# Unit scales on ACT, another order of the first readers, a two-column maximum, and a reordered opening in a conv, GELU and rational MLP kernel

## The chip, the cores and the metric

One core of one Trainium2 chip runs the whole program. The metric is the device time of one execution in microseconds, as the median of several runs; lower is better. The engines are PE (TensorE, with its weight loads PEld), DVE (VectorE), ACT (ScalarE), POOL (GpSimd) and SP (SyncE).

## The reference

```python
# 1. causal 7-tap convolution over the sequence, taps = softmax(weight), one set of taps per head
x_pad = np.concatenate([np.zeros((B, 6, 192)), x], axis=1)
out = np.einsum('hk,bskhg->bshg', w, x_unf)        # x: (2, 4096, 192) -> 8192 tokens x 192
# 2. first MLP: sigmoid-GELU
h = x @ w_in;  g = h * (1 / (1 + np.exp(-1.702 * h)));  x = g @ w_out        # d_ff = 2048
# 3. second MLP: a rational function of h
h = x @ w_in2
P = a[0] + a[1]*h + a[2]*h**2 + a[3]*h**3
Q = 1 + abs(b[0])*abs(h) + abs(b[1])*h**2
out = (P / (Q + 1e-06)) @ w_out2
```

## The kernel before

The 8192 tokens are cut into 16 blocks of 512. The hidden width 2048 is 16 chunks of 128, worked on in eight pairs (index i), one pair to a PSUM tile of 128 x 1024. For precision most products are made from fp16 parts: a tensor is scaled by a power of two, ACT writes its high half (`high_part`, `g1_high`, `split`), DVE writes the rest (`low_part`, `g1_low`), and PE multiplies high and low parts in three terms (`h_main`, `h_side`, `o1_product`). The scale of a tensor comes from its maximum: DVE reduces each partition (`x2_red_part`, in two parts, and L554 joins them), PE turns that column into a row on every partition (`all_max`, L85), DVE takes the maximum of the row (L89) and makes the scale (`scales`).

The main loop goes over j, the block whose second MLP runs, and n1 = j + 1, the block whose first MLP runs.

- **The front part** (`front_groups`, or `front_phase` for j = 0) makes the eight hidden pairs of both MLPs. For the first MLP ACT does the GELU (L524) and the high half (L534), DVE the low half (L538). For the second, `unit` has ACT write |h| (L585) and a linear term (L586), DVE two steps of the polynomial (L587, L588), then `denominator` (L593). The h products lie in a ring of three PSUM tiles (`ps_h`); a tile comes free when its last reader has ended. `front_groups` takes the products in groups of three. The first group was multiplied ahead, at the end of the iteration before: two first-MLP products (`early`, called e0 and e1 here) and one second-MLP product (`second`, called s0). Its readers come in the order e0, s0, e1.
- **The back part** (`back_phase`) multiplies out the first MLP (L496, L506), while POOL makes the convolution of block j + 3 from seven taps (L328, L332; only for j up to 12, since there are 16 blocks). Behind it come x2's maximum and scale, x2's two halves (L345, L348), the group e0, e1, s0 ahead for the next iteration, and part of the second MLP's output products (L485, two passes of fp32). `x2_scales` (L573) makes four small columns, each from the one before it, that `unit` needs as scales of the next block; they are POOL instructions and stand in POOL's queue behind the convolution.
- **The opening** (`prologue`) splits the weights, and runs the first MLP of block 0 with unsplit weights (`o1_whole`: L496 and L506 in turn for each chunk), after which x2 of block 0 is made in the same way. Four `w_out1_split` make the fp16 parts of w_out1; DVE has a step in each (L213), ACT another (L212).
- **The ending** (`ending`) has the last block alone.

The order of each engine's instructions is mostly the order of the text (`manual_schedule`); waits and PSUM slots are placed by the framework.

Of the kernel before, what the change touches and what calls it, by code (L numbers as in the profile page):

```python
# [20 lines left out]
def kernel(  # L21
# [52 lines left out]
    def ps_tile(name):  # L74
        return ps_hs[-1].tile([P, 2, 512], F32, tag="h", name=name)

    def pow2_of(dst, src):
        nc.vector.tensor_scalar(out=dst, in0=src, scalar1=1e-30, scalar2=None, op0=ALU.max)
        nc.vector.tensor_scalar(
            out=dst.bitcast(I32), in0=dst.bitcast(I32), scalar1=EXP_MASK, scalar2=None, op0=ALU.bitwise_and  # L80
        )

    def all_max(red, pm):

        nc.tensor.transpose(out=pm[:, 0, 0:P], in_=red.to_broadcast([P, P]), identity=ident)  # L85

    def all_max_end(pm):
        top = tiny.tile([P, 1], F32, tag="top", name="top")
        nc.vector.tensor_reduce(out=top, in_=pm[:, 0, 0:P], axis=AX.X, op=ALU.max)  # L89
        return top  # L90

    wt8 = const.tile([P, K], F32, name="wt8")
# [261 lines left out]
    def mul(out, in0, f):  # L354
        nc.vector.tensor_scalar(out=out, in0=in0, scalar1=f, scalar2=None, op0=ALU.mult)

    def scales(pm, dst):

        pow2_of(dst[:, 0:1], all_max_end(pm))
        nc.vector.tensor_scalar(  # L360
            out=dst[:, 1:2].bitcast(I32), in0=dst[:, 0:1].bitcast(I32), scalar1=-1, scalar2=(2 * 127 + 14) << 23,
            op0=ALU.mult, op1=ALU.add,
        )
# [157 lines left out]
    def gelu(n, ph, g=None):  # L521
        if g is None:
            g = p2.tile([P, 2 * T], F32, tag="g1", name="g1", bufs=3)
        nc.scalar.activation(  # L524
            out=g, in_=ph.rearrange("p k t -> p (k t)"), func=ACTF.Gelu_apprx_sigmoid, scale=sc1_t[n][:, 3:4]
        )
        return g
# [1 line left out]
    def hl_tile():  # L529
        return p2.tile([P, 2, 2 * T], F16, tag="hl", name="hl1", bufs=8)  # L530

    def g1_high(n, g):
        hl = hl_tile()
        nc.scalar.activation(out=hl[:, 0], in_=g, func=ACTF.Identity, scale=sc1_t[n][:, 4:5])  # L534
        return hl

    def g1_low(n, g, hl):
# [4 lines left out]
    def x2_red(src):  # L542
        red = tiny.tile([P, 2], F32, tag="red2", name="red2")
        for j in range(2):
            x2_red_part(src, j, red)
        return red[:, 0:1]

    def x2_red_part(src, j, red):

        nc.vector.tensor_reduce(  # L550
            out=red[:, j:j + 1], in_=part_of(src, j), axis=AX.X, op=ALU.max, apply_absolute_value=True
        )
        if j:
            nc.vector.tensor_tensor(out=red[:, 0:1], in0=red[:, 0:1], in1=red[:, 1:2], op=ALU.max)  # L554

    def b_consts():

# [9 lines left out]
    def x2_scales(sc, unit):  # L567

        s = sc[:, 2:3]
        for dst, src, f in (  # L570
            (s, sc[:, 0:1], unit), (sc[:, 5:8], ab[:, 1:4], s), (sc[:, 6:8], sc[:, 6:8], s), (sc[:, 7:8], sc[:, 7:8], s)
        ):
            nc.gpsimd.tensor_scalar(out=dst, in0=src, scalar1=f, scalar2=1.0, op0=ALU.mult, op1=ALU.mult)  # L573


    units_t = {}
# [71 lines left out]
    def ending(j, splits):  # L648

        n = j + 1  # L650
        for part in (o1_main, o1_side):
            for i in range(NS):
                o1_product(part, n, i, splits[i])
                if part is o1_main:
                    log(j, i)
        ps_stack.close()
        last = ctx.enter_context(tc.tile_pool(name="ps_last", bufs=1, space=bass.MemoryType.PSUM))
        po_t[1, j] = [last.tile([P, 512], F32, tag=f"l{k}", name="po") for k in range(2)]
        ps_hs.append(ctx.enter_context(tc.tile_pool(name="ps_two", bufs=2, space=bass.MemoryType.PSUM)))
        src = po_t.pop((0, n))  # L660
        each(inverse, j, (0, 1))
        quotient(j, 0)
        o2_chunk(j, 0, 0)
        pm = ps_tile("pm2")
        red = x2_red(src)
        all_max(red, pm)
        o2_chunk(j, 0, 1)
        sc = sc2_t[n] = tiny.tile([P, 24], F32, tag="sc2", name="sc2")
        scales(pm, sc)
        xs = xs2_tiles(n)  # L670
        for p in (0, 1):
            high_part(src, sc[:, 1:2], xs, p)
        quotient(j, 1)
        for p in (0, 1):
            low_part(src, sc[:, 1:2], xs, p)
        each(inverse, j, (2, 3, 4, 5))
        x2_scales(sc, sc1_t.pop(n)[:, 6:7])
        each(quotient, j, (2, 3, 4, 5))
        phs = {}

        def product(i):
            phs[i] = h_product(1, n, i)

        def readers(i):
            pp = hl_tile().rearrange("p two t -> p (two t)").bitcast(F32)
            unit(n, phs.pop(i), pp)

        def own(m, i, groups=range(NG)):
            for k in range(2):
                o2_chunk(m, i, k, groups)  # L690

        first = NS // 2
        own(j, 1)
        rest = [lambda i=i, k=k: o2_chunk(j, i, k) for i in range(2, NS) for k in range(2)]
        product(0)
        rest.pop(0)()
        product(1)
        rest.pop(0)()
        for i in range(NS):
            readers(i)  # L700
            if i < 2:
                inverse(j, i + 6)
            if i + 2 < NS:
                product(i + 2)
            for f in rest[:2 if i > 2 else 1]:
                rest.pop(0)()
            denominator(n, i)
            if i < 2:
                quotient(j, i + 6)
            if i == first + 1:  # L710
                each(log, n, range(first))
            if i == NS - 2:
                each(inverse, n, (0, 1))
                quotient(n, 0)
        for f in rest:
            f()
        each(inverse, n, (2, 3))
        each(quotient, n, (1, 2, 3))
        store(j)
        each(log, n, range(first, NS))  # L720
        for i in range(first, NS):
            inverse(n, i)
            quotient(n, i)
        for i in range(NS - 1):
            own(n, i)
        for groups in (range(0, 2), range(2, 4)):
            own(n, NS - 1, groups)
        store_half(n, 0)
        store_half(n, 1)

    def front_phase(j, n1, extras):

        splits = []
        for i in range(NS):
            if (j, i) in second:
                ph2 = second.pop((j, i))
                ph1 = early.pop((n1, i))
            elif (n1, i) in early:
                ph1, ph2 = early.pop((n1, i)), h_product(1, j, i)
            else:  # L740
                ph1, ph2 = h_product(0, n1, i), h_product(1, j, i)
            g = gelu(n1, ph1)
            unit(j, ph2)
            hl = g1_high(n1, g)
            splits.append(hl)
            if j:
                late_step(j - 1, i)
            for _ in range(2):
                if late_pe:
                    late_pe.pop(0)()  # L750
            g1_low(n1, g, hl)
            denominator(j, i)
            for f in extras.get(i, ()):
                f()
        return splits

    def front_groups(j, n1, extras):

        splits = []
        every = [p for i in range(NS) for p in ((0, n1, i), (1, j, i))]  # L760
        for at in range(0, len(every), 3):
            group = every[at:at + 3]
            if at:
                phs = h_group(group)
            else:
                phs = [early.pop((n1, 0)), second.pop((j, 0)), early.pop((n1, 1))]
            after, late = [], []
            for (m, n, i), ph in zip(group, phs):
                if m:
# [26 lines left out]
    def back_phase(j, n1, n2, conv, splits):  # L796
# [22 lines left out]
        x2_red_part(src, 1, red)  # L819

        def x2_ready():
            scales(pm, sc)
            x2_split(n1, src, sc)

        early[n2, 0], early[n2, 1], second[n1, 0] = h_group(
            ((0, n2, 0), (0, n2, 1), (1, n1, 0)), lambda: all_max(red[:, 0:1], pm), x2_ready
        )
        x2_scales(sc, sc1_t.pop(n1)[:, 6:7])
        each(quotient, j, (0, 1, 2, 3))
# [5 lines left out]
    def prologue():  # L835
# [91 lines left out]
            w_high(("out", 1, c), flat[:, 4 * c * D:4 * (c + 1) * D].bitcast(U32))  # L927
            w_rest(("out", 1, c))

        def o1_whole(i):  # L930

            for k in range(2):
                f = NS * k + i
                w = val_t["out", 0, f // 4].bitcast(F32)[:, f % 4 * D:(f % 4 + 1) * D]
                for part in (o1_main, o1_side):
                    part(0, f, ((w, g0[i], k),))

        flat = wo2.rearrange("p f d -> p (f d)")
# [26 lines left out]
        x_scales(2)  # L965
        x_scale_out(2)
        for i in range(3, NS):
            o1_whole(i)
            if i < 5:
                out2_whole(i - 2)  # L970
            if i < 7:
                w_out1_split((0, 2, 1, 3)[i - 3])
        pm = ps_tile("pm2")
        x2 = po_t.pop((0, 0))
        red = x2_red(x2)
        sc = sc2_t[0] = tiny.tile([P, 24], F32, tag="sc2", name="sc2")
        early[1, 0] = h_product(0, 1, 0, lambda: all_max(red, pm))
        early[1, 1] = h_product(0, 1, 1)
        scales(pm, sc)
        x2_split(0, x2, sc)  # L980
        x2_scales(sc, cst[:, 3:4])
        x_transpose(2)
        out2_whole(3)

# [56 lines left out]
```

## Time and profile before

| | us |
|---|---|
| median of 3 runs (lowest, highest) | 1208.06 (1207.79, 1208.64) |
| the profiled execution | 1209.2 |
| its span | 1207.2 |
| PE busy in the span | 1181.2 |
| DVE, ACT, POOL busy | 944.7, 948.1, 329.0 |

The span is the stretch from the first to the last instruction in the profile; the 2.0 us between it and the profiled execution's time lie outside it. The granted clock of PE was 0.999 of full speed over the span. A row of the timeline gives start and length in us, engine, line, operation, tiles and shapes, how many instructions are merged in it, and in brackets the engine's idle time before it with what ended that. The end of a matmul row is modelled, so the distance from one start to the next start on PE is a better measure than the length.

### The profile page before, as it was taken

The page shows a single profiled execution, that of the slowest core. Times are in us where ns is not written, and L with a number is a line of the kernel's source. Part 1 is how long each engine was busy: PE and PEld are TensorE (multiplying, and loading weights), DVE is VectorE, ACT ScalarE, POOL GpSimd, SP SyncE. Part 2 cuts the span into 40 slices and gives each one's busy share as a digit, 9 for nine tenths or more (in the row PEclk, how much of TensorE's full clock was granted, in tenths as well). Part 3 has the DMA queues.
Part 4 walks back from the last instruction along what each step waited for, and adds up shares of the span by engine and source line. Part 5 has one row for each costly group of instructions (what it writes and reads, how often), then busy time and mean ns, then how long its engine had stood idle before and what let it go on. Part 6 is the DMA issues. An engine that isn't in the chain of part 4 may idle for free. (4 is left out here: it accounts for less than half of the span.)

```text
span 1207.2 us, 24418 instructions
## 1 busy us (share of the span) xinstructions
PE 1181.2 (98%) x10677; PEld 951.4 (79%) x10677; DVE 944.7 (78%) x1050; ACT 948.1 (79%) x969; POOL 329.0 (27%) x340
## 2 busy tenths in 40 slices
PE   9999999999999999999999999999999999999987
PEld 5547787888878788787878878787887878788677
DVE  6979787795968779596886959688695968868684
ACT  3658978779697887969788796978869788796875
POOL 0000704307071340706135080522508053000000
PEclk9999999999999999999999999999999999999999
DMA  8720001010010101001010000101001000000000
GB/s 236 228 56 1 1 1 29 1 28 1 1 28 1 27 1 27 2 1 28 1 27 2 15 14 1 27 2 27 1 1 28 2 14 1 14 1 2 14 1 27
DMA packets 55274, 27.86 MB, mean 23 GB/s; under 512 B 32896, under 2 KB 54400, under 8 KB 54400
## 3 DMA queue, kind: packets, MB, share of 16 engines
q1 hardware_dynamic: 54864, 26.31, 8.4%
q8 instruction: 83, 1.36, 0.5%
q14 instruction: 23, 0.19, 0.0%
q10 hardware_dynamic: 304, 0.00, 0.0%
HBM read 18.97 MB, written 6.29 MB: 21 GB/s over the span
## 5 line engine op out<-in xcount | busy, mean ns | idle before, releaser
L420 PE MATMUL ph<-xs,wm 128*128 128x256 f16 x3072 | 371.3, 273 | 7.3 <-ACT g L524 6.0
L420 PEld LDWEIGHTS <-wm 128*128 128x128 f16 x3072 | 292.1, 98 | 69.2 <-issue 32.2
L485 PE MATMUL po<-wo,pp 128*128 128x192 f32 x1920 | 325.6, 326 | 2.2 <-DVE pp L607 1.6
L485 PEld LDWEIGHTS po<-wo,pp 128*128 128x128 f32 x1920 | 310.1, 190 | 3.9 <-DVE pp L607 1.1
L524 ACT ACTIVATE g<-ph,sc 128x1024 f32<-128x1024 f32 x120 | 133.9, 1116 | 104.7 <-PE ph L434 104.4
L585 ACT ACTIVATE qq<-ph,sc 128x1024 f32<-128x1024 f32 x128 | 142.7, 1115 | 90.7 <-PE ph L434 51.2
L587 DVE TENSOR_TENSOR pp<-pp,ph 128x1024 f32<-128x1024 f32 x120 | 145.8, 1215 | 63.4 <-ACT pp L586 63.0
L434 PE MATMUL ph<-xs,wr 64*128 64x256 f16 x3072 | 187.0, 270 | 3.7 <-DVE hl L588 2.8
L434 PEld LDWEIGHTS <-wr 64*128 64x128 f16 x3072 | 140.6, 94 | 43.5 <-issue 22.6
L328 POOL TENSOR_SCALAR xc<-xt,wt 128x512 f32<-128x512 f32 (+1 forms) x26 | 14.9, 588 | 586.1 <-ACT xt L279 586.1
L607 DVE SCALAR_TENSOR_TENSOR pp<-pp,ab,qq 128x1024 f32<-128x1024 f32 x120 | 163.1, 1389 | 8.8 <-ACT qq L603 8.8
L593 DVE SCALAR_TENSOR_TENSOR qq<-qq,ab 128x1024 f32<-128x1024 f32 x128 | 167.2, 1307 | 0.0
L332 POOL TENSOR_TENSOR xc<-xc,tap 128x768 f32<-128x768 f32 x78 | 163.6, 2097 | 6.5
L538 DVE SCALAR_TENSOR_TENSOR hl<-g,sc,hl 128x1024 f16<-128x1024 f32 x120 | 150.1, 1280 | 14.0 <-ACT hl L534 14.0
L496 PE MATMUL po<-hl,wo 128*128 128x512 f16 x720 | 157.9, 379 | 0.0
L588 DVE SCALAR_TENSOR_TENSOR pp<-pp,sc,ph 128x1024 f32<-128x1024 f32 x120 | 153.6, 1280 | 5.3
L599 ACT ACTIVATE qq<-qq,eps,ab 128x1024 f32<-128x1024 f32 x128 | 146.8, 1228 | 0.2
L586 ACT ACTIVATE pp<-ph,sc 128x1024 f32<-128x1024 f32 x120 | 144.9, 1207 | 0.0
L496 PEld LDWEIGHTS <-wo 128*128 128x128 f16 x720 | 70.3, 98 | 82.0 <-issue 0.4
L534 ACT ACTIVATE hl<-g,sc 128x1024 f16<-128x1024 f32 x120 | 134.0, 1157 | 0.0
L328 POOL TENSOR_SCALAR tap<-xt,wt 128x512 f32<-128x512 f32 (+1 forms) x156 | 127.6, 831 | 6.4
L603 ACT ACTIVATE qq<-qq 128x1024 f32<-128x1024 f32 x128 | 124.9, 1049 | 0.2
(101 smaller groups left out, 730.2 us busy)
## 6 DMA issues: line engine op xcount, KB each, us to landing
raw<-in_moe_w_out_dram SPq DMA_DIRECT2D x8, 768.0 KB, 7.4
out_dram<-on SPq DMA_DIRECT2D x15, 384.0 KB, 2.7
xn<-in_x_dram SPq DMA_DIRECT2D x16, 256.0 KB, 3.4
raw<-in_moe_w_in_dram SPq DMA_DIRECT2D x4, 1024.0 KB, 6.0
xn<-in_x_dram SPq DMA_DIRECT2D x32, 64.0 KB, 3.0
raw<-in_moe_w_in_dram SPq DMA_DIRECT2D x4, 512.0 KB, 7.9
wr<-wr SPq DMA_DIRECT2D x8, 128.0 KB, 2.3
xt<-in_x_dram SPq DMA_DIRECT2D x30, 1.5 KB, 2.6
```

The lines of the kernel that those rows point to most:

```text
L332: nc.gpsimd.tensor_tensor(out=flat_of(c), in0=flat_of(c), in1=flat_of(d), op=ALU.add)
L420: nc.tensor.matmul(out=ph[:, h, k * TH:(k + 1) * TH], lhsT=wm[m][:, a_, f], rhs=xs[:, b_, h * TH:(h + 1) * TH], start=(start and k == 0 an ...
L434: nc.tensor.matmul(out=ph[:, h, k * TH:(k + 1) * TH], lhsT=wr[m][rows, a_, other, f], rhs=xs[rows, b_, :], start=(start and other == 0 and ...
L485: nc.tensor.matmul(out=dst, lhsT=tokens(t, k, g // 2)[:, g % 2 * P:(g % 2 + 1) * P], rhs=rhs, start=(done == 0 and g % 2 == 0 and q == 0), ...
L496: nc.tensor.matmul(out=po_t[0, n][0].rearrange("p (h t) -> p h t", h=2), lhsT=w[:, 0:P], rhs=all_tokens(t, k), start=(at == 1 and q == 0), ...
L538: nc.vector.scalar_tensor_tensor(out=hl[:, 1], in0=g, scalar=sc1_t[n][:, 4:5], in1=hl[:, 0], op0=ALU.mult, op1=ALU.subtract)
L586: nc.scalar.activation(out=pp, in_=h, func=ACTF.Identity, scale=sc[:, 7:8], bias=sc[:, 6:7])
L587: nc.vector.tensor_tensor(out=pp, in0=pp, in1=h, op=ALU.mult)
L588: nc.vector.scalar_tensor_tensor(out=pp, in0=pp, scalar=sc[:, 5:6], in1=h, op0=ALU.add, op1=ALU.mult)
L593: nc.vector.scalar_tensor_tensor(out=qq, in0=qq, scalar=ab[:, 14:15], in1=qq, op0=ALU.add, op1=ALU.mult)
L599: nc.scalar.activation(out=qq, in_=qq, func=ACTF.Ln, scale=ab[:, 15:16], bias=eps)
L607: nc.vector.scalar_tensor_tensor(out=pp, in0=pp, scalar=ab[:, 0:1], in1=qq, op0=ALU.add, op1=ALU.mult)
```

## The change

Five edits:

- `x2_scales` runs on ACT (an Identity with a column as its scale) in place of POOL. It is called in the same places, so on ACT it stands behind x2's high half.
- In `front_groups` the first group's readers come in the order e0, e1, s0.
- In `front_phase` (j = 0 only) the eight `g1_high` run on POOL, and are issued ahead of `unit`.
- L554 is dropped; `all_max` turns both columns of `red` (two transposes), and L89 reduces 256 elements in place of 128 where x2's maximum is made.
- In the opening the last two chunks' `o1_main` come ahead of their `o1_side`, the first part of x2's maximum stands between them, and the last `w_out1_split` stands behind x2's halves and scales.

```diff
     def all_max(red, pm):
-        nc.tensor.transpose(out=pm[:, 0, 0:P], in_=red.to_broadcast([P, P]), identity=ident)
-    def all_max_end(pm):
+        for c in range(red.shape[1]):
+            nc.tensor.transpose(
+                out=pm[:, 0, c * P:(c + 1) * P], in_=red[:, c:c + 1].to_broadcast([P, P]), identity=ident
+            )
+    def all_max_end(pm, cols=1):
...
-    def g1_high(n, g):
+    def g1_high(n, g, by_pool=False):
         hl = hl_tile()
-        nc.scalar.activation(out=hl[:, 0], in_=g, func=ACTF.Identity, scale=sc1_t[n][:, 4:5])
+        if by_pool:
+            nc.gpsimd.tensor_scalar(
+                out=hl[:, 0], in0=g, scalar1=sc1_t[n][:, 4:5], scalar2=1.0, op0=ALU.mult, op1=ALU.mult
+            )
+        else:
+            nc.scalar.activation(out=hl[:, 0], in_=g, func=ACTF.Identity, scale=sc1_t[n][:, 4:5])
...
-        if j:
-            nc.vector.tensor_tensor(out=red[:, 0:1], in0=red[:, 0:1], in1=red[:, 1:2], op=ALU.max)
...
-            nc.gpsimd.tensor_scalar(out=dst, in0=src, scalar1=f, scalar2=1.0, op0=ALU.mult, op1=ALU.mult)
+            nc.scalar.activation(out=dst, in_=src, func=ACTF.Identity, scale=f)
...
             g = gelu(n1, ph1)
+            hl = g1_high(n1, g, True)
+            splits.append(hl)
             unit(j, ph2)
-            hl = g1_high(n1, g)
-            splits.append(hl)
...
-        every = [p for i in range(NS) for p in ((0, n1, i), (1, j, i))]
+        every = [(0, n1, 0), (0, n1, 1), (1, j, 0), (1, j, 1)]
+        every += [p for i in range(2, NS) for p in ((0, n1, i), (1, j, i))]
...
-                phs = [early.pop((n1, 0)), second.pop((j, 0)), early.pop((n1, 1))]
+                phs = [early.pop((n1, 0)), early.pop((n1, 1)), second.pop((j, 0))]
...
         for i in range(3, NS):
-            o1_whole(i)
+            o1_whole(i, (o1_main, o1_side) if i < NS - 2 else (o1_main,))
             if i < 5:
                 out2_whole(i - 2)
-            if i < 7:
+            if i < 6:
                 w_out1_split((0, 2, 1, 3)[i - 3])
+        red = tiny.tile([P, 2], F32, tag="red2", name="red2")
+        x2_red_part(po_t[0, 0], 0, red)
+        for i in range(NS - 2, NS):
+            o1_whole(i, (o1_side,))
         pm = ps_tile("pm2")
         x2 = po_t.pop((0, 0))
-        red = x2_red(x2)
+        x2_red_part(x2, 1, red)
...
         x2_scales(sc, cst[:, 3:4])
+        w_out1_split(3)
         x_transpose(2)
```

## Rows read from the trace of the kernel before

**Rows 1.** The page's first part: busy time, share, instructions of each engine.
```profile
PE 1181.2 (98%) x10677; PEld 951.4 (79%) x10677; DVE 944.7 (78%) x1050; ACT 948.1 (79%) x969; POOL 329.0 (27%) x340
```

**Rows 2.** Waits of PE alone: line, waited for, us in total, times, longest.
```profile
PE ph L420 <- ACT g L524: 6.0, 13, 1.2
PE po L485 <- PE ph L420: 0.6, 1, 0.6
```

**Rows 3.** Waits of all engines, the one row of ACT on POOL.
```profile
ACT qq L585 <- POOL sc L573: 25.1, 13, 2.8
```

**Rows 4.** Timeline, 985 to 1030 us: a back part's end and the next front part.
```profile
992.98 1.05 PE L420 MATMUL ph<-xs,wm 128*128 128x256 f16 x8
...
993.55 0.46 DVE L554 TENSOR_TENSOR red<-red 128x1 f32<-128x1 f32 x1
...
994.06 0.32 PE L85 MATMUL pm<-ident,red 128*128 128x128 f32 x1
...
994.22 1.91 PE L420 MATMUL ph<-xs,wm 128*128 128x256 f16 x16
...
1000.22 1.28 ACT L524 ACT_TABLE_LOAD   x1
1001.52 1.11 ACT L524 ACTIVATE g<-ph,sc 128x1024 f32<-128x1024 f32 x1
...
1004.21 0.27 POOL L573 TENSOR_SCALAR sc<-sc,sc 128x1 f32<-128x1 f32 x1
1004.51 1.11 ACT L585 ACTIVATE qq<-ph,sc 128x1024 f32<-128x1024 f32 x1 [1.88 <-POOL sc L573]
...
1006.70 1.11 ACT L524 ACTIVATE g<-ph,sc 128x1024 f32<-128x1024 f32 x1
...
1007.86 1.47 PE L420 MATMUL ph<-xs,wm 128*128 128x256 f16 x12 [0.42 <-ACT g L524]
...
1008.16 1.28 DVE L588 SCALAR_TENSOR_TENSOR pp<-pp,sc,ph 128x1024 f32<-128x1024 f32 x1
...
1009.26 2.14 PE L434 MATMUL ph<-xs,wr 64*128 64x256 f16 x36
```

**Rows 5.** Timeline, 1050 to 1082 us: the same place for j = 13, without convolution.
```profile
1063.28 1.05 PE L420 MATMUL ph<-xs,wm 128*128 128x256 f16 x8
...
1064.16 0.27 PE L85 MATMUL pm<-ident,red 128*128 128x128 f32 x1
1064.27 1.91 PE L420 MATMUL ph<-xs,wm 128*128 128x256 f16 x16
```

**Rows 6.** Timelines of the opening, 48 to 90 us.
```profile
73.93 2.87 DVE L213 SCALAR_TENSOR_TENSOR wo<-v,wsc,wo 128x768 f16<-128x768 f32 x3
...
77.98 0.32 PE L85 MATMUL pm<-ident,red 128*128 128x128 f32 x1 [1.31 <-DVE red L554]
...
80.23 1.12 ACT L524 ACTIVATE g<-ph,sc 128x1024 f32<-128x1024 f32 x1
```

**Rows 7.** Timeline of the front part of j = 0, 88 to 160 us.
```profile
105.41 1.11 ACT L524 ACTIVATE g<-ph,sc 128x1024 f32<-128x1024 f32 x1
...
106.81 1.28 DVE L538 SCALAR_TENSOR_TENSOR hl<-g,sc,hl 128x1024 f16<-128x1024 f32 x1
...
117.33 1.49 PE L420 MATMUL ph<-xs,wm 128*128 128x256 f16 x12 [0.73 <-DVE pp L588]
```

**Rows 8.** Prices: POOL and DVE timelines from 125 to 145 us, and groups by form.
```profile
126.49 0.48 POOL L328 TENSOR_SCALAR xc<-xt,wt 128x256 f32<-128x256 f32 x1
126.94 0.70 POOL L328 TENSOR_SCALAR tap<-xt,wt 128x512 f32<-128x512 f32 x1
...
142.51 1.82 POOL L332 TENSOR_TENSOR xc<-xc,tap 128x768 f32<-128x768 f32 x1
143.05 2.36 DVE L607 SCALAR_TENSOR_TENSOR pp<-pp,ab,qq 128x1024 f32<-128x1024 f32 x1
...
L849 ACT ACTIVATE warm<-eps 128x1 f32<-128x1 f32 x1 | 0.2, 202 | 0.0
```

## What the change will do, told before it was run

> **What bounds the kernel now.** I read the page's busy times first, then the waits of PE, then the timeline at each place where PE waits. PE is busy 98% of the span [rows 1], so 26 us of 1207.2 are idle on PE, and only a change that removes PE's idle time, or PE's work, can show. Work moved between ACT, DVE and POOL is worth what it does to PE's waits. The longest entry in PE's waits is the GELU of ACT: 6.0 us in 13 pieces [rows 2]. The number 13 recurs: 13 times ACT waits for POOL's unit scales, 25.1 us in all [rows 3], and 13 blocks have a convolution on POOL. The timeline of one such place shows the whole chain [rows 4]. ACT does e0's GELU at 1001.52, then stands 1.88 us before L585, until POOL, late from the convolution, writes the first scale at 1004.21; s0's two readers and only then e1's GELU follow (1006.70 to 1007.81), and at 1007.86 PE starts a product that waited 0.42 us for the PSUM tile of e1. So the wait is POOL's lateness, handed on by the order e0, s0, e1.
>
> A second, hidden loss: eight matmuls, then the turn of x2's maximum. With POOL at work the turn starts 1.08 us after the first of the eight (994.06 - 992.98), without it 0.88 (1064.16 - 1063.28) [rows 4, 5]. DVE's L554, which joins the two columns, took 0.46 us and ended at 994.01, right ahead of the turn. The 0.20 us is called busy by the page, since ends of matmuls are modelled.
>
> **The change, part by part.**
>
> *Scales on ACT and the order e0, e1, s0.* These go together. e1's GELU then ends two GELUs after 1001.52, plus d, the time of the four scale instructions that now stand ahead of it on ACT: 1001.52 + 2.22 + d = 1003.74 + d. PE wanted e1's tile at 1007.86 - 0.42 = 1007.44, so d may be 3.7 us before that wait returns. What is late next is s0's tile: the third product of the group takes it. L585 would start at 1003.74 + d, where it started at 1004.51; L588, the last reader, ended at 1009.44, and so ends at 1008.67 + d. PE wants that tile after two thirds of the 36 side matmuls, which start 0.42 earlier than 1009.26: 1008.84 + 1.43 = 1010.27. So d must stay under 1.6 us. No row shows this instruction on ACT. The nearest is an ACT operation on one column, 0.202 us [rows 8]; POOL's own took 0.27 [rows 4]. Between 0.4 (overlapped) and 1.1 (four of POOL's), I take 0.9: four at 0.2 and a little for each reading what the one before wrote. All of that range is under 1.6, so the wait goes and nothing of it returns. Queued behind the four on ACT are four sigmoids, a table load and the GELU; all that is d, counted above. In the ending they come behind four sigmoids, and there ACT waits for PE anyway. Sum: **-6.0 us**, 13 places, nothing given back.
>
> *Two columns turned.* L554 goes, and with it 0.20 us at the 12 places with POOL at work (in the thirteenth, j = 0, I find no such loss): -2.4. PE gets one more turn in each of 14 blocks. One cost 0.11 (1064.27 - 1064.16) to 0.16 (994.22 - 994.06) [rows 4, 5]; I take 0.12, near the undisturbed one: +1.7. L89 reads 256 elements in place of 128, which makes DVE's chain some 0.13 longer, against an earlier start of 0.1 to 0.2; x2's halves are wanted by PE well after that. In the ending the same swap is even. Sum: **-0.7 us** (bounds -1.3 if one more turn hides at 0.08, and -0.2 at 0.16).
>
> *The opening.* PE waits 1.31 us for x2's maximum, because DVE works through three splits first [rows 6]. One of them leaves (2.87 / 3 = 0.96) and L554 with it (0.46 beside POOL [rows 4], less here; I take 0.15): the turn can come 1.1 earlier, less 0.1 for the second turn: -1.0. Taking the last mains ahead of the last sides makes PE ready sooner too, but DVE remains last. What stands against it: ACT gets the four scales and perhaps the high part of the moved split (0.9) ahead of block 0's first GELU, which before ran at 80.23, as soon as x2's halves were written. PE wants that tile about 81.4, which leaves nothing or 0.9 of a wait; I take half of it. Sum: **-0.5 us** (bounds -1.0 and +0.1). The moved split's own result is read a whole front part later.
>
> *Eight high halves on POOL in j = 0.* ACT is relieved of 8 operations; its last one goes from ahead of the transposed input, logs and sigmoids, which so start about 1 us earlier, and that frees a wait of PE of 0.6 before the first output product [rows 2]: -0.6. But DVE, not ACT, is last in this part: the one real wait of PE is 0.73 us for L588 [rows 7]. POOL takes 0.70 us for 512 columns and 0.48 for 256, so by that slope about 1.13 for 1024 [rows 8]. DVE's low half comes more than 5 us after the GELU, so it does not wait for POOL's result. What it meets is POOL at work: L607, two SBUF operands, started beside POOL's add and took 2.36 where 1.28 is usual, and ended 1.08 late [rows 8]. L538 and L593 have two SBUF operands as well. By the times of the GELUs, POOL would start shortly before L538 about once or twice in the stretch from 100 to 117 us that DVE fills (the GELU of i = 4 ends at 106.52, L538 of i = 3 starts at 106.81 [rows 7]); after one such delay the two fall out of step and POOL works beside L587 and L588, which read PSUM. So 0 to 1.6 us of DVE time reach PE; I take 0.8. Sum: **+0.2 us** (bounds -0.6 and +1.0).
>
> The Trainium skill, "SBUF — State Buffer", section "Who interferes with whom", has a rule that speaks against this edit: a DVE instruction with two SBUF inputs and a GpSimd instruction that reads SBUF exclude each other, and the loser blocks fully. The 2.36 us row agrees. Taken at its full price it is the first rival below.
>
> **Sum:** -6.0 - 0.7 - 0.5 + 0.2 = -7.0. The profiled span goes from 1207.2 to 1200.2, and with the 2.0 us around it that execution from 1209.2 to 1202.2. It lay 1.1 above the median of the runs, so the median goes from 1208.06 to **1201.1**. With all bounds together the main case reaches from -8.9 to -5.1: 1199.2 to 1203.0.
>
> **The rivals.**
>
> *POOL and DVE block each other all through j = 0's front part.* Each high half costs DVE its 1.13 us: 9.0. I take it that 2 of them fall into waits that DVE has anyway; 7 us come on the path: 1201.1 - 0.8 + 7 = 1207.3, no change that can be measured. For it: two in four DVE operations there have two SBUF operands, and DVE is last. Against it: an operation that meets no such one costs nothing, and one delay shifts the phase.
>
> *The wait returns at s0's tile.* If ACT's four scales take d = 2 us, 0.4 us comes back at 13 places, 5 us: 1206.3. No row on ACT this narrow is near 0.5 us.
>
> *Slower.* Two ways by one place. Should each scales chain make ACT load another table and the next sigmoid load it back (1.28 us each [rows 4]), d is 0.9 + 2.6 = 3.5, 1.9 over the limit at 13 places, 25 us: about 1226. It makes the kernel slower than before from d of about 2.1 us. Against it: x2's high half is an Identity too and stands between sigmoids without a load. The same would follow if the framework gave the second product s0's tile and not e1's (wanted at 1007.44, free at 1009.57, 2.1 us x 13); but in the kernel before the second product already takes e1's, though e1 was read last on ACT.
>
> *The change does not do what it says:* the order of an engine in the framework differs from the text (it does at the seam of opening and loop) and ACT meets the GELU first and the scales late. Then s0 waits as now, but e1 does not: the 6.0 still go. This changes nothing in the forecast.
>
> **How the numbers follow.** The main case has 0.72, POOL against DVE 0.13, the returned wait 0.08, slower 0.04, and 0.03 is for more gain than counted. A measurement of this kernel tells about 0.2%, 2.4 us, from no change; so faster means under 1205.6. The main case and half of what lies between it and the first two rivals are faster: 0.87. No measurable change 0.08, slower 0.05. To hold 8 in 10 the range takes the main case, 1.5 us beneath it for terms I did not see, and the nearer part of the two milder rivals: 1197.5 to 1205.0.
>
> **What would show it.** Right: PE's waits on ACT's GELU at L420 gone from the list, no ACT wait on POOL at L585, a block of the loop some 0.5 us shorter, the turn 0.88 us after the first of the eight matmuls, x2's turn in the opening near 76.9. Wrong: a wait of L434 or L420 on L588 at the start of front parts (d over 1.6), more table loads than before, DVE's L538 or L593 in j = 0 well above 1.28 us and PE's wait for L588 there above 2 us. The forecast fails most likely in j = 0, where POOL's cost is worked out from two shapes and its meeting with DVE from the times of one run.

## The result and the profile after

The changed kernel takes **1195.08 us** in the median (1194.39 to 1197.33, 5 runs) against 1208.06 (1207.58 to 1208.64, 5 runs): a ratio of 0.9897 [0.9883, 0.9912], 13.0 us less. The forecast of 1201.1 had the sign right; the gain is nearly double what it told, and the time lies below the stated range, which began at 1197.5. The profiled execution took 1194.39 us with a span of 1192.6, where that of before had 1209.2 and 1207.2: the executions differ by 14.8, their spans by 14.6.

The first part of the page, which answers to [rows 1] (busy time, share, instructions):

```profile
PE 1174.6 (98%) x10693; PEld 952.3 (80%) x10693; DVE 939.7 (79%) x1034; ACT 954.6 (80%) x1025; POOL 318.3 (27%) x284
```

PE's idle time is now 18 us, where it was 26. That is 8 of the 14.6 us by which the spans differ; the rest was booked as busy. The waits of PE after, which answer to [rows 2] (line, waited for, total us, times, longest):

```profile
PE po L488 <- DVE hl L613: 4.4, 2, 2.5
PE ph L437 <- DVE hl L594: 2.6, 2, 1.3
PE po L488 <- DVE pp L613: 1.7, 2, 1.0
...
PE pm L86 <- DVE red L558: 0.9, 1, 0.9
```

Both rows of [rows 2] are gone, and so is the row of [rows 3]: no engine waits for POOL's unit scales any more. What stands first is the ending, which was there before with the same 4.4 us. The timeline of the place of [rows 4], a back part's end and the next front part (start, duration, engine, line, operation, output<-inputs, count):

```profile
909.71 1.05 PE L423 MATMUL ph<-xs,wm 128*128 128x256 f16 x8
...
910.59 0.38 PE L86 MATMUL pm<-ident,red 128*128 128x128 f32 x2
...
910.81 1.91 PE L423 MATMUL ph<-xs,wm 128*128 128x256 f16 x16
...
913.04 0.29 ACT L579 ACTIVATE sc<-sc,sc 128x1 f32<-128x1 f32 x1
913.36 0.30 ACT L579 ACTIVATE sc<-ab,sc 128x3 f32<-128x3 f32 x1
913.69 0.62 ACT L579 ACTIVATE sc<-sc 128x2 f32<-128x2 f32 x2
914.22 3.88 ACT L609 ACTIVATE qq<-qq 128x1024 f32<-128x1024 f32 x4
...
919.41 2.12 ACT L527 ACTIVATE g<-ph,sc 128x1024 f32<-128x1024 f32 x2
...
922.54 2.78 PE L423 MATMUL ph<-xs,wm 128*128 128x256 f16 x24
924.92 1.28 DVE L594 SCALAR_TENSOR_TENSOR pp<-pp,sc,ph 128x1024 f32<-128x1024 f32 x1
925.26 2.14 PE L437 MATMUL ph<-xs,wr 64*128 64x256 f16 x36
```

The two GELUs follow each other (919.41, x2), and PE runs both products as one piece of 24, where [rows 4] has twelve, a wait, and twelve. From the first product to the sides it takes 925.26 - 922.54 = 2.72 us. Before it was 1009.26 - 1005.96 = 3.30, with the start of the twelve that run ahead of the row at 1007.86 in [rows 4]:

```profile
1005.96 1.47 PE L420 MATMUL ph<-xs,wm 128*128 128x256 f16 x12
```

The true loss per block is therefore 0.58 us, though [rows 4] shows 0.42 in brackets. The eight matmuls ahead of the turn now take 910.59 - 909.71 = 0.88, as forecast.

Two distances are used below. A **block** is the time from one set of L506 (after: L509) matmuls to the next, in blocks with a convolution. The **first stretch** runs from the turn for the weights' maximum (58.96 before, 58.13 after) to the first side matmuls of the front part of j = 1; it holds the opening, j = 0 and the start of j = 1. Measured from that turn, it is free of the loads before it, which vary.

| kernel | block | first stretch | median | ratio to before |
|---|---|---|---|---|
| before | 71.09 | 97.18 | 1208.06 | |
| after | 70.38 | 92.95 | 1195.08 | 0.9897 [0.9883, 0.9912] |

### The profile page after: what moved, and what is told of

It is laid out like the page before. It is cut to its first block, busy times and chain, and to the rows that moved or that the text cites. A ratio compares the mean times of both kernels' runs of the same rounds, so it can differ in the third digit from the quotient of the medians.

```text
span 1192.6 us, 24394 instructions
## 1 busy us (share of the span) xinstructions
PE 1174.6 (98%) x10693; PEld 952.3 (80%) x10693; DVE 939.7 (79%) x1034; ACT 954.6 (80%) x1025; POOL 318.3 (27%) x284
## 4 chain that ended last, share of the span: by engine, by line
PE 91%; DVE 5%; ACT 3%; issue 1%; POOL 0%; ACTq 0%; POOLq 0%
PE ph L423 27%; PE po L488 26%; PE ph L437 14%; PE po L499 13%; PE po L509 7%; PE pc L321 2%; ACT qq L605 1%; PE pt L275 1%; DVE pp L613 1%; DVE hl L593 0%; PE pm L86 0%; DVE wm L216 0%; DVE qq L599 0%; ACT hl L592 0%; ACT qq L591 0%
## 5 line engine op out<-in xcount | busy, mean ns | idle before, releaser
L423 PE MATMUL ph<-xs,wm 128*128 128x256 f16 x3072 | 369.3, 273 | 0.7 <-ACT hl L527 0.4
L423 PEld LDWEIGHTS <-wm 128*128 128x128 f16 x3072 | 291.5, 98 | 60.5 <-issue 24.2
L488 PE MATMUL po<-wo,pp 128*128 128x192 f32 x1920 | 325.6, 326 | 1.7 <-DVE pp L613 1.7
L488 PEld LDWEIGHTS po<-wo,pp 128*128 128x128 f32 x1920 | 310.1, 190 | 3.1 <-DVE pp L613 1.3
L594 DVE SCALAR_TENSOR_TENSOR pp<-pp,sc,ph 128x1024 f32<-128x1024 f32 x120 | 153.6, 1280 | 4.3
L546 DVE SCALAR_TENSOR_TENSOR hl<-g,sc,hl 128x1024 f16<-128x1024 f32 x120 | 151.6, 1292 | 6.4 <-ACT hl L542 6.4
L542 ACT ACTIVATE hl<-g,sc 128x1024 f16<-128x1024 f32 x112 | 125.0, 1161 | 0.0
```

What stands on the lines that cost most here:

```text
L423: nc.tensor.matmul(out=ph[:, h, k * TH:(k + 1) * TH], lhsT=wm[m][:, a_, f], rhs=xs[:, b_, h * TH:(h + 1) * TH], start=(start and k == 0 an ...
L488: nc.tensor.matmul(out=dst, lhsT=tokens(t, k, g // 2)[:, g % 2 * P:(g % 2 + 1) * P], rhs=rhs, start=(done == 0 and g % 2 == 0 and q == 0), ...
L546: nc.vector.scalar_tensor_tensor(out=hl[:, 1], in0=g, scalar=sc1_t[n][:, 4:5], in1=hl[:, 0], op0=ALU.mult, op1=ALU.subtract)
L594: nc.vector.scalar_tensor_tensor(out=pp, in0=pp, scalar=sc[:, 5:6], in1=h, op0=ALU.add, op1=ALU.mult)
```

## The experiments

**Before once more.** Unedited, for what differs between executions of one kernel.

> The kernel before, unchanged, a second profile. Theory now: what the change does not touch differs between two executions, above all the first 30 us (loads) and the last 27 us (granted clock 0.94 in the first profile of before, 1.00 in that of after). Then the blocks of the loop stay at 71.1 us to 0.05, the second product of a front part again starts 1.90 us after the first, and only the ends of the span move, by 1 to 2 us. Rival: the block length itself varies between executions, by 0.2 us or more, and the 0.73 us that a block got shorter is partly that.

One run, 1208.18 us; block 71.07, first stretch 97.15. The two traces of the kernel before agree to 0.02 and 0.03 us. What doesn't repeat is ahead of and behind it: the weights' turn came at 58.24, where the profile of before has 58.96, and over all kernels it came between 57.62 and 59.05, with nothing in common between the early ones.

**The order alone, the scales alone.** The one edit on the kernel before is

```
every = [(0, n1, 0), (0, n1, 1), (1, j, 0), (1, j, 1)] + (pairs from i = 2 as before)
phs = [early.pop((n1, 0)), early.pop((n1, 1)), second.pop((j, 0))]
```

and the other

```
- nc.gpsimd.tensor_scalar(out=dst, in0=src, scalar1=f, scalar2=1.0, op0=ALU.mult, op1=ALU.mult)
+ nc.scalar.activation(out=dst, in_=src, func=ACTF.Identity, scale=f)
```

> The kernel before with the order e0, e1, s0 alone; the scales stay on POOL. Theory now: the wait ahead of a front part's second product goes wholly, since e1's GELU no longer stands behind POOL, and s0's last reader ends where it did, 0.7 us ahead of its need: start to start 1.31 us in place of 1.90, a block 0.59 shorter (70.5), 12 x 0.59 + 1.34 = 8.4 us in all: 1199.7. Prediction's size of the wait: 6.0, 1202. Rival: POOL's lateness then shows at s0's tile, the third product waits, and most of the gain is lost: above 1205.

> The kernel before with the scales on ACT alone; the order stays e0, s0, e1. Theory now: e1's GELU starts at 1006.70 - 1.88 + about 1.2 for the four scales = 1006.0 and ends at 1007.1, just ahead of its need at 1007.27, so this alone also takes nearly the whole wait: a block 0.5 to 0.59 shorter, 1200 to 1201. Rival: the two edits work only together, and this one leaves half of the wait: 1204.

The order gave 1200.12 us, 0.9934 [0.9919, 0.9949]; the scales gave 1198.28, 0.9925 [0.9909, 0.9942]. Blocks are 70.50 in both, first stretches 95.82 and 95.97. Timeline of the order alone at the place of [rows 4]:

```profile
992.50 2.12 ACT L524 ACTIVATE g<-ph,sc 128x1024 f32<-128x1024 f32 x2
...
995.20 0.26 POOL L573 TENSOR_SCALAR sc<-sc,sc 128x1 f32<-128x1 f32 x1
995.49 1.11 ACT L585 ACTIVATE qq<-ph,sc 128x1024 f32<-128x1024 f32 x1 [0.87 <-POOL sc L573]
...
996.95 2.78 PE L420 MATMUL ph<-xs,wm 128*128 128x256 f16 x24
```

ACT still waits 0.87 us for POOL, but PE's 24 products run in one piece. With the scales alone the second GELU comes after s0's readers and is still just in time: it ends at 998.38, and the second twelve are due at 997.43 + 1.32 = 998.75.

```profile
997.26 1.12 ACT L524 ACTIVATE g<-ph,sc 128x1024 f32<-128x1024 f32 x1
997.43 2.78 PE L420 MATMUL ph<-xs,wm 128*128 128x256 f16 x24
```

So either edit alone removes the whole wait, and the two don't add. What they are worth: 12 blocks by 0.58 (70.50 against 71.07 and 71.09), and 1.3 at the start of j = 1 (the longest entry, 1.2, of [rows 2]), 8.2 us in all. Directly, from the weights' turn to the last block's L506, the order alone is 8.0 and 8.3 us shorter than the two traces of before, the scales alone 8.1 and 8.4. The two medians are 1.8 apart all the same: from the last block's L506 to the end the trace of the order alone takes 79.8 us and that of the scales alone 78.0, by the granted clock (last section).

**The high halves of j = 0 back on ACT**, behind the unit step as before, and in another kernel ahead of it, as the changed kernel has them on POOL. On the kernel after:

```
- hl = g1_high(n1, g, True)
+ hl = g1_high(n1, g)          (in the first of the two also: behind unit(j, ph2))
```

> The changed kernel with the eight high halves of j = 0 back on ACT and back behind the unit. Theory now: the edit gains about 1.7 us (1.0 in the front part, 0.7 at the first output product), because ACT is free earlier and the PSUM tile of the last first-MLP product then comes from a GELU and not from DVE's L588: 1196.8 here, and the wait on L588 comes back. Prediction's theory: it costs 0.2, so this kernel is 0.2 faster than the changed one. Rival: the gain in j = 0's front part came from the reordered opening, and stays: 1195.1.

> The changed kernel with j = 0's eight high halves on ACT, but issued ahead of the unit as in the change: the order of the edit without its engine. Theory now: what gains is ACT's free time, so this gives nothing of the 1.7 us, and more likely costs: each unit's two readers start 1.1 us later behind the high half, and the wait on L588 grows: from the weights' turn to the first second-product sides of j = 1 94.7 us or more (92.95 in the changed kernel, 94.68 with highs on ACT behind the unit). Rival: the order alone makes the framework give the last first-MLP product a GELU's tile; then part of the gain comes here too: 93.7.

1197.92 us, 0.9917 [0.9902, 0.9931], and 1198.08, 0.9923 [0.9906, 0.9939]. First stretches are 94.68 and 95.09, against 92.95. So POOL's highs are worth 1.7 us against highs on ACT in the old order, and 2.1 against highs on ACT in the new one, where I had them cost 0.2. The wait of [rows 7] returns, here with highs on ACT behind unit:

```profile
112.85 1.48 PE L423 MATMUL ph<-xs,wm 128*128 128x256 f16 x12
...
115.06 1.48 PE L423 MATMUL ph<-xs,wm 128*128 128x256 f16 x12 [0.73 <-DVE pp L594]
...
119.61 0.88 PE L275 MATMUL pt<-ident,xn 128*128 128x128 f32 x6 [0.23 <-ACT g L527]
```

In the changed kernel, by ACT's, DVE's and PE's timelines there:

```profile
113.21 3.06 PE L423 MATMUL ph<-xs,wm 128*128 128x256 f16 x24
...
113.62 1.13 ACT L527 ACTIVATE g<-ph,sc 128x1024 f32<-128x1024 f32 x1
...
114.57 1.28 DVE L594 SCALAR_TENSOR_TENSOR pp<-pp,sc,ph 128x1024 f32<-128x1024 f32 x1
...
114.80 0.71 PE L423 MATMUL ph<-xs,wm 128*128 128x256 f16 x5
```

PE begins the second twelve at 114.80, while L594 is at work until 115.85. It does not wait for it: the semaphore that this product waits on in the trace is ACT's, where it was DVE's before. The framework gave the product another PSUM tile, one that ACT releases. That tile was not ready either: the GELU ended at 114.75, and from the first twelve to the second it takes 1.59 us where 1.32 is free, a wait of 0.27 that the list of waits leaves out. With the highs on ACT but ahead of the unit step, the product takes such a tile too, but PE waits at other places:

```profile
82.93 2.84 PE L321 MATMUL pc<-xt,diag 128*128 128x512 f32 x6 [0.36 <-ACT xt L282]
...
113.64 1.48 PE L423 MATMUL ph<-xs,wm 128*128 128x256 f16 x12
115.34 1.47 PE L423 MATMUL ph<-xs,wm 128*128 128x256 f16 x12 [0.22 <-ACT g L527]
...
143.75 2.54 PE L488 MATMUL po<-wo,pp 128*128 128x192 f32 x14 [0.98 <-DVE pp L613]
```

Four places tell the three kernels apart. Each row is the distance from the start of twelve L423 matmuls to the start of what comes next on PE, which is 1.32 us where nothing waits:

| from twelve L423 to | highs on ACT, behind unit | on ACT, ahead of unit | on POOL, ahead (after) |
|---|---|---|---|
| the first products of the opening's convolution (L321) | 1.32 | 1.85 | 1.32 |
| the second twelve | 2.21 | 1.70 | 1.59 |
| the transposed input (L275) | 1.71 | 1.47 | 1.32 |
| the first output product (L488) | 1.89 | 2.47 | 1.32 |

At the second twelve the order ahead of the unit step saves 0.51 us with the highs still on ACT, and POOL another 0.11. With that order on ACT the first high half stands ahead of the copies of the transposed input, which costs 0.53 at L321, and the first output product waits longer still. Against the changed kernel the four rows make 1.58 and 1.94 of the 1.7 and 2.1 us.

**One column turned**, on the kernel after:

```
-  for c in range(red.shape[1]): transpose(out=pm[:, 0, c * P:(c + 1) * P], in_=red[:, c:c + 1] ...)
+  transpose(out=pm[:, 0, 0:P], in_=red[:, 0:1] ...)
+  if j: nc.vector.tensor_tensor(out=red[:, 0:1], in0=red[:, 0:1], in1=red[:, 1:2], op=ALU.max)
```

> The changed kernel with L554's maximum back and one column turned. Theory now: a block with a convolution gets 0.12 to 0.14 us longer (70.50), the two blocks without one 0.11 shorter, and the opening's turn comes 0.2 later by L554 and costs 0.1 less: 1196.6. Prediction's theory: 0.08 a block, 0.7 in all, 1195.8. Rival: the join of the columns is hidden with the new order of readers, and the block stays at 70.38.

1197.22 us, 0.9913 [0.9898, 0.9928]; block 70.50, first stretch 93.16, the last block, without convolution, 69.47 against 69.57 in the changed kernel. Two turns are worth 0.12 in each of 12 blocks and 0.2 in the opening, and cost 0.1 where POOL is idle: 1.5 us.

**The opening undone**: the four edits there reverted, all else as after.

> The changed kernel with the opening as it was (last split ahead of x2, mains and sides in turn). Theory now: from the weights' turn to the first side product of block 0's second MLP 23.4 us in place of 22.34, the rest as in the changed kernel: 1196.2. Prediction's theory: 0.5 us: 1195.6. Rival: the front part of j = 0 is bound by ACT and DVE and takes the 1.1 us back before its end: 1195.1.

1196.09 us, 0.9906 [0.9891, 0.9921]. x2's turn comes 18.49 us after the weights' turn (after: 75.70 - 58.13 = 17.57), and the first stretch is 93.92. All of the 0.92 stays. The turn in the opening undone, and in the changed kernel:

```profile
77.10 0.65 PE L86 MATMUL pm<-ident,red 128*128 128x128 f32 x2 [0.79 <-DVE red L558]
```

```profile
74.03 1.01 DVE L216 SCALAR_TENSOR_TENSOR wo<-v,wsc,wo 128x768 f16<-128x768 f32 x1
...
74.97 1.01 DVE L558 TENSOR_REDUCE red<-po 128x1 f32<-128x512 f32 x2
...
75.70 0.66 PE L86 MATMUL pm<-ident,red 128*128 128x128 f32 x2 [0.90 <-DVE red L558]
...
76.19 0.60 PE L423 MATMUL ph<-xs,wm 128*128 128x256 f16 x4
...
78.60 1.11 ACT L527 ACTIVATE g<-ph,sc 128x1024 f32<-128x1024 f32 x1
```

The bracket is longer after (0.90 against 0.79), though x2 comes earlier: PE too is ready earlier. A bracket alone would have told the wrong sign.

**A longer chain on ACT.** Four, and in another kernel two, more operations of the same kind stand ahead of the four scales; they write columns that nobody reads.

```
+ for c in range(4):      (two: range(2))
+     nc.scalar.activation(out=sc[:, 17 + c:18 + c], in_=sc[:, 16 + c:17 + c] if c else sc[:, 0:1], func=ACTF.Identity, scale=unit)
```

> The changed kernel with four more small operations on ACT ahead of the four scales (they write columns that nobody reads), so that d goes from 1.2 to about 2.5 us. Prediction's theory: what is late next is s0's tile, from d of 1.6 us: the third product of each front part's second group waits about 0.8 us, on DVE's L594, at 13 or 14 places: a block near 71.2, 1206. Rival: another tile is given or the reader is ahead of my reckoning, and up to d of 2.5 us nothing waits: 1195.

> The changed kernel with two more small operations ahead of the four scales, d about 1.8 us. With four more d was 2.35 and each block 0.85 longer, so the limit by that run is 1.5 and a block should be 0.3 longer: 70.68, about 1199 to 1200. By the prediction's limit of 1.6 it is 0.2: 70.58. Rival: the wait does not grow with d one for one, and the block is at 70.38 or above 70.8.

Four more: 1209.14 us (10 runs), 1.001 [1.0001, 1.002], blocks 71.23. That is 3 us above what was expected, though the blocks are as told; 1.0 us of it is lost in the opening and j = 0, where the four also stand ahead of the copies of the transposed input. Two more: 1200.15 (one run), blocks 70.58. The waits of PE and the timeline, four more:

```profile
PE ph L437 <- DVE pp L598: 9.5, 14, 0.7
```

```profile
923.95 1.27 ACT L577 ACTIVATE sc<-sc,sc 128x1 f32<-128x1 f32 x4
...
926.30 3.88 ACT L613 ACTIVATE qq<-qq 128x1024 f32<-128x1024 f32 x4
...
937.00 1.28 DVE L598 SCALAR_TENSOR_TENSOR pp<-pp,sc,ph 128x1024 f32<-128x1024 f32 x1
...
938.34 0.83 PE L437 MATMUL ph<-xs,wr 64*128 64x256 f16 x12 [0.68 <-DVE pp L598]
```

With d = 926.30 - 923.95 = 2.35, PE waits where the forecast's second rival put the wait, at s0's tile for its last reader (there L588), and the whole gain is lost. A block grows by 0.85 at d = 2.35 and by 0.20 at d = 1.69 (918.21 - 916.52 in the kernel with two more), so the wait begins at d = 2.35 - 0.85 = 1.50, or 1.69 - 0.20 = 1.49. The changed kernel has d = 914.22 - 913.04 = 1.18: it lies 0.3 us, one such operation, under that limit.

**Every high half on POOL twice**, the second time over the first.

```
+ for _ in range(2):
      nc.gpsimd.tensor_scalar(out=hl[:, 0], in0=g, scalar1=sc1_t[n][:, 4:5], scalar2=1.0, ...)
```

> The changed kernel with each of j = 0's eight high halves done twice on POOL (the second writes the same values), 2.25 us a pair. First rival of the prediction: POOL and DVE's two-operand instructions shut each other out, DVE is last, and each further 1.12 us of POOL costs DVE as much: 8 x 1.1 = 9 us, 1204. Theory now: of eight single ones one met DVE, for 0.73 us, and PE did not feel it; the second ones will meet L546 or L599 in most of the eight pairs, but PE feels only what outruns DVE's slack in the ring: 1 to 4 us, 1196 to 1199, with L546 or L599 rows near 2 us in the timeline. If PE feels nothing, 1195.1.

1197.26 us, 0.9911 [0.9894, 0.9927]; first stretch 94.38, 1.4 more than after. PE's, DVE's and POOL's timelines in j = 0:

```profile
90.04 2.01 DVE L547 SCALAR_TENSOR_TENSOR hl<-g,sc,hl 128x1024 f16<-128x1024 f32 x1
101.64 2.06 DVE L600 SCALAR_TENSOR_TENSOR qq<-qq,ab 128x1024 f32<-128x1024 f32 x1
107.31 1.48 PE L423 MATMUL ph<-xs,wm 128*128 128x256 f16 x12 [0.94 <-DVE pp L595]
110.86 4.53 POOL L539 TENSOR_SCALAR hl<-g,sc 128x1024 f16<-128x1024 f32 x2 [3.80 <-ACT g L527]
115.92 6.61 POOL L539 TENSOR_SCALAR hl<-g,sc 128x1024 f16<-128x1024 f32 x4 [0.53 <-ACT g L527]
```

Eight more POOL operations (9 us of POOL) make DVE lose 0.7 to 0.8 us twice, and one product waits 0.94 us for L595. This is not the product of the kernels above, which takes ACT's tile here too, but one 8.6 us ahead of it, which is released by DVE in every kernel here and elsewhere in time. For the rest POOL gives way: two operations, 2.33 us elsewhere, spread over 4.53.

## Why the prediction was right and wrong

| step | told | measured | by |
|---|---|---|---|
| scales on ACT, order e0, e1, s0 | -6.0 | -8.2 | order alone, scales alone |
| two columns turned, in the loop | -0.7 | -1.3 | one column |
| the opening, with its second column | -0.5 | -1.1 | opening undone, one column |
| eight highs on POOL | +0.2 | -1.7 | highs on ACT |
| sum | -7.0 | -12.3 | |

Two terms put the time out of the range, both the same way: the highs on POOL, with the wrong sign and 1.9 us off, and PE's wait for the GELU, 2.2 too small. From the weights' turn to the last block's L506 the changed kernel is 12.7 us shorter than the profile of before, and 12.4 shorter than the second trace; the medians differ by 13.0. The rest is outside the change's reach as far as the traces tell. The weights' turn came 0.83 earlier in the profile of after (58.96 - 58.13), as it came 0.72 earlier in the second trace of before. From the last block's L506 to the end the profile of after is 1.1 shorter: its last 112 matmuls took 18.47 us in place of 20.15, by the granted clock (below), while what follows them took 3.8 in place of 3.4. 12.7, 0.8 and 1.1 are the 14.6 by which the spans differ.

**Scales and order: the mechanism right, the term too small.** The wait went at all 13 places, and the chain was read rightly: POOL's lateness, handed on by the order. The size was taken from the list of waits, 6.0. But a bracket is counted from the end of the matmul before, and the ends are modelled. For the turn I applied that caution and measured from start to start; for the largest term of the sum I didn't. By the starts of [rows 4] it was to be had: 1005.96 (twelve matmuls) to 1007.86 are 1.90, against 1.32 for 12 of the 24 that follow each other in the changed kernel, 0.16 more than the bracket at each of 13 places: 2.1 us, nearly all that this term was too small.

**The price on ACT: too low, and nothing lost by it.** I took d = 0.9, with bounds to 1.1; it was 1.18. Each operation takes 0.29 to 0.31, not the 0.20 of [rows 8], an operation of another function that has no column as its scale; which of the two makes the difference was not tried. The limit that I worked out, 1.6, was 1.5. The rival stood 0.3 us away, and the longer chains show that its place, and its price at 13 or 14 places, were right. There are 50 table loads before and after, and in the loop the four scales stand where they were told.

**Two columns: 0.12 in place of 0.06 a block.** The gain at the turn was right, 0.20. By starts, two turns take 0.22 us to the next matmuls (910.59 to 910.81), where one took 0.16 beside POOL [rows 4] and 0.11 without [rows 5]. One turn more thus costs 0.06 at the 12 places that gain and 0.11 where POOL is idle; I took 0.12, the price without POOL, for all. 0.20 less 0.06 is 0.14, where the blocks show 0.12.

**The opening: the whole, not half.** x2's turn comes 17.57 us after the weights' turn, where it was 77.98 - 58.96 = 19.02: 1.45 earlier, told 1.1. The second turn takes back 0.33 here (75.70 to 76.19 is 0.49, a single one takes 0.16), told 0.1. Half of a 0.9 wait for ACT's queue was set against it. The framework put the GELU between the scales (78.42 the first scale, 78.60 the GELU), and no wait followed. The bound of +0.1 was a slip: -1.0 with the whole of the 0.9 is -0.1.

**The highs on POOL: the step that failed in sign.** Three pieces. POOL's own price was right: 1.12 measured, 1.13 told. The first rival, POOL and DVE blocking each other all through, didn't come; the changed kernel has a slowed DVE there once, beside the fourth of POOL's eight high halves:

```profile
99.24 1.12 POOL L538 TENSOR_SCALAR hl<-g,sc 128x1024 f16<-128x1024 f32 x1 [4.75 <-ACT g L527]
99.42 2.01 DVE L546 SCALAR_TENSOR_TENSOR hl<-g,sc,hl 128x1024 f16<-128x1024 f32 x1
```

The 0.7 us did not reach PE: the twelve ahead of 114.80 start 55.08 us after the weights' turn, and 55.05 with the highs on ACT. I had taken 0.8. Twice the POOL work cost PE only 1.4 us, so the first rival's full price is not what a kernel pays when the pair meets seldom. The Trainium skill ("SBUF — State Buffer", "Who interferes with whom") says that a DVE instruction with two SBUF inputs contends with a GpSimd instruction that reads SBUF. The row agrees, with 2.01 us in place of 1.28.

And "DVE, not ACT, is last in this part" was wrong as a reason that relief of ACT buys no more than the 0.6 at the output product. The wait was for DVE's L588 only because of which PSUM tile the product was given. After, it was given one that ACT releases: 0.6 of the gain, put at nothing in the sum. The transposed input gave 0.4 more, also put at nothing, and the wait before the first output product the 0.6 that was told. The order did most of the first (0.5 of 0.6): the two kernels with the highs on ACT differ in it alone, and have DVE's tile with the highs behind the unit step and ACT's with the highs ahead. So do all others: ACT's tile in the seven kernels with the highs ahead, DVE's in the five with them behind. What in the framework makes the order choose the tile stays open. Relief of ACT did the rest: with the new order on ACT all is lost again, not at the tile but at the other three places.

No kernel here beats the changed one.

## What to carry to other kernels

Size a wait of PE by the distance from start to start against the same matmuls where they run freely, for every term and the largest first: the bracket in the list of waits left out 0.16 us of 0.58 at each place, and a wait of 0.27 was not listed at all. When a chain is moved to another engine, work out the limit at which the next wait returns and measure how far off it is: here the room was 0.3 us, one small operation, and two more no longer fitted. Where the framework hands out buffers, the engine that a product waits for can change when two lines of another engine change places, so relief of an engine that "isn't last" is to be bounded by the wait for the one that is, not put at nothing. Test an order and an engine apart, and compare place by place: one sum from the start mixes a tile that came free early with a delay elsewhere.

## What the runs showed of the hardware

In some executions, of whatever kernel, the last 112 matmuls took 20.1 us in place of 18.5. These are the wait ahead of them and their first stretches, before and then after (stretch, us, busy us of PE, PEld, DVE, ACT, POOL, granted clock as a share, DMA share, GB/s):

```profile
1181.10:1183.70 2.60, 0.05 (x2) 0.02 (x1) 2.60 (x4) 2.57 (x3) 0.00 (x0) 1.00 0.45 151
1183.70:1185.70 2.00, 2.00 (x9) 2.00 (x10) 2.00 (x2) 2.00 (x3) 0.00 (x0) 0.69 0.00 0
1185.70:1187.70 2.00, 2.00 (x8) 2.00 (x8) 0.32 (x1) 1.98 (x3) 0.00 (x0) 0.50 0.00 0
1187.70:1189.70 2.00, 2.00 (x14) 2.00 (x13) 0.03 (x1) 1.99 (x3) 0.00 (x0) 0.96 0.00 0
```

```profile
1167.70:1170.30 2.60, 0.05 (x2) 0.03 (x1) 2.60 (x4) 2.57 (x3) 0.00 (x0) 1.00 0.45 151
1170.30:1172.30 2.00, 2.00 (x12) 2.00 (x13) 2.00 (x2) 2.00 (x3) 0.00 (x0) 1.00 0.00 0
1172.30:1174.30 2.00, 2.00 (x15) 2.00 (x14) 0.31 (x1) 1.98 (x3) 0.00 (x0) 1.00 0.00 0
```

Both have the same two waits of PE for DVE, 1.84 and 2.55 us, the second of them right ahead of these matmuls. In the first the clock is at 0.50 in one of the stretches (1.2 GHz in place of 2.4) once PE works again; in the second it stays at 1.00. Over the last 27 us the mean was 0.94 in both profiles of before, the order alone, both highs on ACT, one column, two more and highs twice, and 1.00 in after, the scales alone, the opening undone and four more. What decides it was not found: it doesn't follow the ending's code, which is the same in after and in the kernels with the highs on ACT, whose edit is in j = 0. Of the five runs of the changed kernel three have a mean clock of 1.000, of the 27 of before that were taken beside the experiments three, so part of the 13.0, at most these 1.7 us, may be this and not the change; the 12.4 and 12.7 of the distances are free of it.

Small operations on ACT, each reading what the one before wrote, start 0.32 to 0.33 us apart (913.04, 913.36, 913.69). POOL and DVE slow each other, either way: DVE's L546 took 2.01 us in place of 1.28 beside one POOL high half, and two POOL high halves took 4.53 in place of 2.33 while DVE ran its two-operand instructions.
